# Replanning the attention half of a fused attention and expert kernel, with the first pair's rotation and the weight words in PSUM

## The chip, the cores and the metric

One core of a Trainium2 chip runs one program. Its engines are TensorE (PE in the profile), VectorE (DVE), ScalarE (ACT), GpSimd (POOL) and SyncE (SP), which here only issues transfers. The metric is the device time of one execution in microseconds; lower is better.

## What is computed

Attention over 4 sequences, 8 heads, 576 tokens and 64 columns a head, with rotated q and k, then two expert layers on the 2304 tokens of 512 columns. Everything is in fp32.

```
q_rot, k_rot = rotate(q), rotate(k)          # x1*cos - x2*sin, x1*sin + x2*cos
scores = (q_rot @ k_rot.T) / 8
attn   = exp(scores - max);  attn = attn / (sum(attn) + 1e-9)
x = (attn @ v)                               # heads side by side: 2304 x 512
x = (silu(x @ w_gate) * (x @ w_val)) @ w_out # d_ff 1536
out = relu(x @ w_in)**2 @ w_out2             # d_ff 2048
```

The host hands over q and k transposed, pair by pair, with a second copy whose halves are swapped, and a table of cosines and signed sines, so that a rotation is two products and a sum.

## The kernel before

The work has two parts. The first is attention: 16 pairs of heads (`NG`, four pairs for each of four sequences), with the first two of twelve chunks of the first expert layer done for three of the five token blocks in between, as filler for TensorE. The second part is the rest of the two expert layers; its instructions are ordered by the framework, from the loops at L749 to L812.

Precision. A product in fp32 is made of three products of a high and a low half (`mm3`, L261). The high half is a rounded copy (type fp32r), the low one the difference. For scores, k is split into `kh` and `kl`, q into `qa` (high half in a head's own 64 partitions, low half in the other 64) and `qz` (high half, zeros elsewhere), so a score tile of 128 queries and half of the 576 keys is two matmuls.

One pair g goes through these steps:

- `add_prep` (L450): SP loads q and k into `rot` (four buffers) and v. GpSimd multiplies both copies by the table in one operation of 1152 columns (L467) and adds the halves (L468). Pair 0 is done on VectorE instead, in two halves of 288 tokens (`PARTS`), and its loads carry rank -1000 so that they come first.
- `add_kq` (L481): pair 0 is split by ScalarE (L494, L499), VectorE (L495, L500) and GpSimd (L503). For later pairs ScalarE rounds (L509), GpSimd subtracts (L511), and transfers issued by SP place the pieces (L523).
- `add_scores` (L525): nine tiles of scores into PSUM (`s`, two buffers), each followed by VectorE's row maximum (L549) and ScalarE's exponential with row sums (L551). The ninth tile holds the last 64 tokens of both heads.
- `add_values` (L555): TensorE transposes the exponentials (L572) into `pt` (two PSUM buffers), ScalarE or VectorE copies them out (L564, L566), TensorE multiplies by v into `av` (L605, L608). The ninth tile is divided by its sums before it is transposed: GpSimd adds 1e-9 (L578), VectorE takes the reciprocal (L579), GpSimd scales (L580). The others are divided after the product, through a transposed copy of the reciprocals (L616, L625, L627). The result is split into high and low (L633, L635).
- `add_weight` (L648): six weight tiles are loaded raw as 64-bit words and unpacked to fp32 by `unpack_steps` (L218): ScalarE scales the upper word (L221), VectorE shifts the lower word (L222), joins the two (L223) and adds the sign (L224), ScalarE rounds (L225), GpSimd subtracts (L226). L222 to L224 work between the SBUF tiles `wa` and `wp`. The second part unpacks its 62 tiles by the same function.
- `add_filler` (L671): for three token blocks, two chunks of the first expert layer, accumulated in the one PSUM bank `mm` (L680).

The order. All these are handed to `Plan` as operations with an engine, an estimate in ns, what they read and write, and a rank. `Plan.order` (L89) runs a list schedule over the engines with those estimates: an engine that is idle takes the ready operation of lowest rank, buffers of a ring (`places`) are taken as they come free, and what comes out is the order in which the instructions are emitted. On each engine they then run in that order, a late one holding those behind it. A rank is the pair's number plus an offset for its kind (`RANK`, L21); `RANK0` adds to it for the first four pairs and is empty. For TensorE the estimates are doubled where the plan takes the clock to be halved (L162), `STAY` is what a change between scores and transposes costs in rank and `SWITCH` in ns. SP's issues are planned as operations too, with a fixed time to landing (`hold`). Before all this, VectorE and GpSimd clear some tiles (L411 to L420). The scaled table `csq` (L712) is made by ScalarE with rank -900.

## Time and profile before

| | us |
|---|---|
| median of three runs | 1168.81 |
| lowest and highest | 1167.99, 1169.2 |
| the profiled execution | 1169.47 |
| its span, first to last instruction | 1167.6 |

| engine | busy us of the span | share |
|---|---|---|
| TensorE matmuls | 1113.6 | 95% |
| TensorE weight loads | 930.4 | 80% |
| VectorE | 577.5 | 49% |
| GpSimd | 520.5 | 45% |
| ScalarE | 478.2 | 41% |

The shares are means over two parts that have different limits, so they are read by stretch. A bracket at the end of a row of the timeline holds the idle time of that engine just before it and what ended it. A row that starts with PE is a matmul; matmuls overlap, so the distance of two starts tells the pace, not the length of one.

### The profile page before, as it was taken

To read this page: it belongs to the slowest core of one execution; us is meant where nothing else is said; L and a number is where in the kernel's file an instruction comes from. 1 tells how busy PE (TensorE), PEld (TensorE's weight loads), DVE (VectorE), ACT (ScalarE), POOL (GpSimd) and SP (SyncE) were. 2 spreads that over 40 slices of the span, in tenths; PEclk is the share of its full clock that TensorE was granted. 3 is DMA by queue.
4 is the path that set the end of the run, shared out by engine and by line. 5 is a ranking of instruction groups with operands and counts; after the bars stand their busy time and mean duration, and the time that the engine had idled before them with its cause. 6 is when DMAs were issued, how large, how long until landed. Compare 5 with 4: busy or idle time off the path is not lost.

```text
span 1167.6 us, 16632 instructions
## 1 busy us (share of the span) xinstructions
PE 1113.6 (95%) x6336; PEld 930.4 (80%) x6336; DVE 577.5 (49%) x920; ACT 478.2 (41%) x980; POOL 520.5 (45%) x434
## 2 busy tenths in 40 slices
PE   2788999999999999999999999999999999999998
PEld 2666777778787888888888888888888888888886
DVE  6787555556653664635537355471144236233222
ACT  4567656666664532313223133353353224223121
POOL 4999866867423442313223134472244234224121
PEclk9999999999999999999999999999999999999999
DMA  8665566564424830202102021020021013000112
GB/s 272 191 164 166 165 166 187 149 192 121 105 83 136 315 104 25 90 1 73 36 19 91 1 72 36 19 91 1 1 89 57 1 36 91 1 1 1 64 28 73
DMA packets 61105, 102.45 MB, mean 88 GB/s; under 512 B 11104, under 2 KB 37216, under 8 KB 60128
## 3 DMA queue, kind: packets, MB, share of 16 engines
q1 hardware_dynamic: 60448, 97.18, 28.1%
q0 software_dynamic: 576, 4.19, 1.0%
q8 instruction: 50, 0.82, 0.3%
q14 instruction: 31, 0.25, 0.1%
HBM read 67.17 MB, written 12.06 MB: 68 GB/s over the span
## 4 chain that ended last, share of the span: by engine, by line
PE 77%; POOL 9%; DMA 5%; DVE 3%; issue 2%; ACT 2%; SPq 1%; POOLq 0%; DVEq 0%; ACTq 0%
PE mm L262 22%; PE mm L263 22%; PE mm L264 21%; POOL rot L467 4%; PE pt L572 3%; PE mm L680 3%; PE av L605 3%; PE s L543 3%; DMA rot<-in_k_dram 2%; POOL rot L468 2%; SPq L523 1%; DMA v<-in_v_dram 1%; DVE wp L223 1%; POOL kl L511 1%; ACT p L551 1%
## 5 line engine op out<-in xcount | busy, mean ns | idle before, releaser
L277 POOL TENSOR_TENSOR h<-s,h 128x512 fp32r<-128x512 f32 (+1 forms) x80 | 96.2, 1202 | 181.5 <-ACT h L276 178.5
L277 POOL TENSOR_TENSOR h<-hf,h 128x512 fp32r<-128x512 f32 (+1 forms) x54 | 66.5, 1231 | 151.0 <-ACT h L276 150.9
L543 PE MATMUL s<-kh,qa 128*128 128x288 f32 x320 | 95.7, 331 | 35.1 <-ACT p L551 21.5
L296 DVE TENSOR_TENSOR s<-r,mm 128x512 f32<-128x512 f32 (+1 forms) x80 | 50.6, 632 | 147.0 <-POOL h L277 75.1
L549 DVE TENSOR_REDUCE nm<-s 128x1 f32<-128x576 f32 x144 | 105.7, 752 | 32.1 <-PE s L543 30.0
L551 ACT ACTIVATE p<-s,nm 128x576 f32<-128x576 f32 x144 | 105.6, 736 | 33.4 <-DVE nm L549 31.0
L263 PE MATMUL mm<-wo,h 128*128 128x512 f32 x288 | 110.8, 389 | 0.0
L572 PE MATMUL pt<-ident,p 128*128 128x128 f32 (+1 forms) x720 | 103.8, 280 | 7.3 <-POOL p L580 3.4
L262 PE MATMUL mm<-wo,h 128*128 128x512 f32 x288 | 109.5, 389 | 0.0
L572 PEld LDWEIGHTS pt<-ident,p 128*128 128x128 f32 (+1 forms) x720 | 81.0, 137 | 23.9 <-issue 6.0
L226 POOL TENSOR_TENSOR wi<-wa,wi 128x512 fp32r<-128x512 f32 x36 | 47.1, 1309 | 108.9 <-ACT wi L225 108.9
L543 PEld LDWEIGHTS s<-kh,qa 128*128 128x128 f32 x320 | 60.9, 197 | 42.0 <-ACT p L551 27.3
L223 DVE SCALAR_TENSOR_TENSOR wp<-wa,wp 128x512 uint32<-128x512 uint32 x68 | 64.0, 942 | 61.1 <-ACT wa L221 61.0
L264 PE MATMUL mm<-wo,h 128*128 128x512 f32 x288 | 93.2, 389 | 0.0
L294 ACT ACTIVATE r<-mm 128x512 f32<-128x512 f32 (+1 forms) x80 | 43.8, 548 | 116.6 <-PE mm L264 116.0
L566 DVE COPY pc<-pt 128x512 f32<-128x512 f32 (+1 forms) x102 | 67.9, 682 | 42.7 <-PE pt L572 41.9
L285 DVE SCALAR_TENSOR_TENSOR th<-th,mm 128x512 f32<-128x512 f32 (+1 forms) x54 | 33.8, 627 | 105.9 <-ACT th L283 105.9
L543 PE MATMUL s<-kl,qz 128*128 128x288 f32 x288 | 83.7, 305 | 1.2 <-DVE kl L495 1.2
L276 ACT ACTIVATE h<-s 128x512 fp32r<-128x512 f32 (+1 forms) x80 | 47.1, 589 | 79.4 <-DVE s L296 79.4
L605 PE MATMUL av<-pc,v 128*64 128x256 f32 x640 | 76.1, 384 | 0.0
L264 PE MATMUL mm<-h,wo 128*128 128x512 f32 (+1 forms) x200 | 72.6, 369 | 0.0
L263 PE MATMUL mm<-h,wo 128*128 128x512 f32 (+1 forms) x200 | 72.6, 368 | 0.0
(198 smaller groups left out, 2780.2 us busy)
## 6 DMA issues: line engine op xcount, KB each, us to landing
raw<-in_moe_w_out_dram SPq DMA_DIRECT2D x26, 512.0 KB, 3.5
rot<-in_k_dram SPq DMA_DIRECT2D x15, 576.0 KB, 4.6
rot<-in_q_dram SPq DMA_DIRECT2D x15, 576.0 KB, 3.8
kh<-rot SPq DMA_DIRECT2D x60, 144.0 KB, 2.5
raw<-in_moe_w_in_dram SPq DMA_DIRECT2D x16, 512.0 KB, 3.6
raw<-in_moe_w_gate_dram SPq DMA_DIRECT2D x10, 512.0 KB, 3.5
raw<-in_moe_w_val_dram SPq DMA_DIRECT2D x10, 512.0 KB, 3.5
qa<-rot SPq DMA_DIRECT2D x30, 144.0 KB, 2.6
```

What stands on the lines that cost most here:

```text
L223: lambda: nc.vector.scalar_tensor_tensor(out=p(), in0=a(), scalar=3, in1=p(), op0=ALU.logical_shift_left, op1=ALU.bitwise_or),
L262: nc.tensor.matmul(ps, lhsT=ah, rhs=bh, start=first, stop=False)
L263: nc.tensor.matmul(ps, lhsT=ah, rhs=bl, start=False, stop=False)
L264: nc.tensor.matmul(ps, lhsT=al, rhs=bh, start=False, stop=last)
L277: nc.gpsimd.tensor_tensor(out=h[:, 1, :n], in0=hf[:, :n], in1=h[:, 0, :n].bitcast(F32), op=ALU.subtract)
L296: nc.vector.tensor_tensor(out=s[:, :n], in0=r[:, :n], in1=a, op=ALU.mult)
L543: nc.tensor.matmul(ps()[:, i, :HS], lhsT=a, rhs=w, start=y == 0, stop=y == len(prods) - 1)
L549: plan.add("DVE", 755, lambda ps=ps, nm=nm: nc.vector.tensor_reduce(out=nm(), in_=ps()[:, :, :HS], axis=AX.XY, op=ALU.max, negate=True), [ ...
L551: plan.add("ACT", 930, lambda x=x, ps=ps, nm=nm, p=p: nc.scalar.activation(p().rearrange("p (a b) -> p a b", a=2), ps()[:, :, :HS], AF.Exp ...
L566: nc.vector.tensor_copy(dst()[:kk], pt()[:kk, :n])
L572: nc.tensor.matmul(pt()[:kk, off + n * 128:off + n * 128 + 128], lhsT=p()[:, c * 128:c * 128 + kk], rhs=ident, is_transpose=True)
L605: nc.tensor.matmul(av()[h * 64:h * 64 + 64, 0:256], lhsT=vt()[:, h, c], rhs=pcs[c]()[:, h * 256:h * 256 + 256], start=c == 0, stop=c == 4)
```

## The change

Seven things are altered, all in the first part.

1. The rotation of pair 0 is three operations for each of q and k and each half: a product within `rot`, a product into PSUM (`pt` for k; `av` and `mm` for q), and a sum in PSUM. ScalarE and VectorE split k and q from there.
2. A dummy exponential on a tile that GpSimd clears is issued on ScalarE before the plan. The making of `csq` also waits for the last high piece of q (head 1, second half).
3. The table is loaded through ScalarE's queue. Pair 1's q and k get rank -9000 on SP, right behind pair 0's.
4. In `add_weight` the tile `p` is the PSUM bank `mm` in place of `wp`. The second part's `load_split` keeps `wp`.
5. The ninth tile's scaling is done by ScalarE or VectorE, as the plan picks, in place of GpSimd. So is the copy of `av` (L619), and pair 1's rotation may go to VectorE (`SHARE`).
6. A transpose takes the SBUF buffer of its copy at the same time (`claim`).
7. The plan: the model of TensorE's clock is gone; operations with `port` wait in the plan for one another between VectorE and GpSimd; transfers land by a rate (`RATE`, `LAND`); some estimates change; and all ranks are new, with `RANK0` for the first four pairs and `RANK1` for the first two.

```diff
-RANK = dict(ld=9.786, rope=-1.966, k=-2.118, lo=-1.665, dup=3.173, v=-2.497, s=-5.055, mx=-3.798, ex=-1.062, pt=-4.839, hi=-0.71, av=1.151, rec=-0.195, x=29.148, out=-3.224, fin=-38.149, scale=-8.913, w=0.449, dw=0.542, fill=-3.274, df=4.236)
-RANK0 = dict()
+RANK = dict(ld=176.169, rope=77.556, k=133.052, lo=-64.241, dup=130.669, v=-12.083, s=27.238, mx=100.534, ex=60.673, pt=-5.142, hi=45.754, av=95.071, rec=-6.745, x=179.568, out=-4.367, fin=-49.53, scale=-159.05, w=28.595, dw=27.25, fill=63.17, df=5.551)
+FIRST = dict(rope=((-997, -1000), (-995, -999)), k=((-998.5, -995.9), (-998, -995.8)), q=((-996.9, -995.7), (-994.9, -994.8)))
+SHARE = (1,)
+RANK0 = dict(ld=-0.835, rope=-50.984, ...)
+RANK1 = dict(ld=53.997, rope=-27.634, ...)
...
-    SWITCH = 54
-    STAY = 13.92
+    SWITCH = 80
+    STAY = 67.654
...
-                    if eng == "PE":
-                        if int((now + self.PHASE) / self.TICK) > tick:
...
-                        ns *= 1 if full else 2
+                    if ops[i]["port"] and eng == "DVE" or eng == "Pool":
+                        ns += max(0, held["Pool" if eng == "DVE" else "DVE"] - now)
+                        held[eng] = now + ns
+                    if ops[i]["size"]:
+                        moved = max(moved, now + self.LAND) + ops[i]["size"] / self.RATE
+                        hold = moved - now - ns
...
+        first = sm.tile([128, 1], F32, name="first", bufs=1)
+        nc.gpsimd.memset(first, 0.0)
+        nc.scalar.activation(first, first, AF.Exp)
...
+                    if g == 0 and i == 1:
+                        plan.add("ACT", 600, lambda c0=c0, c1=c1: nc.scalar.dma_start(out=cs()[:, :, c0:c1], in_=rope[:, :, c0:c1]), [], [(cs, n)], -1e4 + n, size=1024 * w)
+                    plan.add("SP", 600, lambda ...: nc.sync.dma_start(out=x()[:, :, c0:c1], in_=(q, k)[i][b, j][:, :, c0:c1]),
+                             [], [(x, n)], (-1e4 + n + 0.1 * (1 - i) if g == 0 else -9e3 if g == 1 else g + rk("ld", g) + 0.1 * (1 - i)), size=1024 * w)
...
+                        at0 = FIRST["rope"][n][i]
+                        y = buf("pt", [128, 512], bufs=2, pool=pp) if i else buf(("av", "mm")[n], [128, 512], pool=pp)
+                        for e in range(2):
+                            o = (lambda x=x, c0=c0, c1=c1: x()[:, 0, c0:c1]) if e == 0 else (lambda y=y, w=w: y()[:, :w])
+                            plan.add("DVE", dve(w, 150), lambda ...: nc.vector.tensor_tensor(out=o(), in0=x()[:, e, c0:c1], in1=cs()[:, e, c0:c1], op=ALU.mult),
+                                     [(cs, n)] + ([] if e == 0 else [(x, n)]), [(x, n)] if e == 0 else [y], at0, port=True)
+                        plan.add("DVE", dve(w, 150), lambda ...: nc.vector.tensor_tensor(out=y()[:, :w], in0=y()[:, :w], in1=x()[:, 0, c0:c1], op=ALU.add), [(x, n)], [y], at0)
...
-                            plan.add("Pool", pool_ns(cols), lambda fn=fn: fn(nc.gpsimd), csk if i else [csq], [(x, n)], at + 0.01 * (1 - i))
+                        ways = [("Pool", pool_ns(cols), lambda fn=fn: fn(nc.gpsimd))]
+                        if g in SHARE:
+                            ways.append(("DVE", dve(cols, 100), lambda fn=fn: fn(nc.vector)))
+                        plan.add_any(ways, csk if i else [csq], [(x, n)], at + 0.01 * (1 - i), port=True)
...
-            plan.add("Pool", 900, lambda: nc.gpsimd.tensor_scalar(pr(), pr(), rr(), None, ALU.mult), [rr], [pr], at)
+            plan.add_any([("ACT", 680, lambda: nc.scalar.activation(pr(), pr(), AF.Copy, scale=rr())),
+                          ("DVE", 400, lambda: nc.vector.tensor_scalar(pr(), pr(), rr(), None, ALU.mult))], [rr], [pr], at, port=True)
...
-            raw, a, p = buf("h", [128, 1024], U32, 4, hp), buf("wa", [128, 512], U32, 1, tp), buf("wp", [128, 512], U32, 1, tp)
+            raw, a, p = buf("h", [128, 1024], U32, 4, hp), buf("wa", [128, 512], U32, 1, tp), buf("mm", [128, 512], U32, pool=pp)
...
-        plan.add("ACT", act(2 * S), lambda: nc.scalar.activation(csq(), cs(), AF.Copy, scale=0.125), csk, [csq], -900)
+        plan.add("ACT", act(2 * S), lambda: nc.scalar.activation(csq(), cs(), AF.Copy, scale=0.125), csk + [(pair[0]["qa"], (1, 0, 1))], [csq], -900)
```

The ranks that the prediction speaks of are those of `RANK`: on TensorE `s` for scores, `pt` for transposes, `av` for the products with v, `fill` for the filler (to which four for each sequence and a step of up to `df` are added).

## Rows read from the trace of the kernel before

**Rows 1.** Busy time by stretch, the whole span but its last 6 us.

```profile
core 0: us, PE busy (x) PEld busy (x) DVE busy (x) ACT busy (x) POOL busy (x), PEclk, DMA share, GB/s
0.00:13.16 13.16, 0.00 (x0) 0.00 (x0) 7.27 (x16) 4.15 (x7) 2.62 (x12) 1.00 0.81 257
13.16:30.00 16.84, 9.53 (x36) 7.87 (x36) 13.12 (x20) 10.26 (x25) 11.82 (x11) 1.00 0.78 270
30.00:53.00 23.00, 16.88 (x150) 13.69 (x148) 16.13 (x21) 12.26 (x29) 21.38 (x14) 1.00 0.81 217
53.00:70.30 17.30, 13.56 (x83) 11.66 (x84) 15.00 (x22) 12.01 (x29) 14.92 (x12) 0.80 0.50 130
70.30:130.00 59.70, 52.74 (x446) 41.98 (x444) 44.98 (x71) 41.94 (x101) 57.19 (x46) 1.00 0.62 175
130.00:372.70 242.70, 232.19 (x1859) 190.46 (x1859) 140.85 (x249) 150.76 (x357) 140.56 (x122) 0.99 0.51 140
372.70:1161.60 788.90, 788.35 (x3770) 664.71 (x3768) 339.24 (x525) 246.86 (x440) 272.05 (x222) 1.00 0.16 53
```

**Rows 2.** TensorE's waits up to 380 us: total us, times, longest.

```profile
PE s L543 <- ACT p L551: 21.5, 16, 4.5
...
PE pt L572 <- POOL p L580: 3.4, 3, 1.7
```

**Rows 3.** The chain that ended last: start us, us, what; four and eight score matmuls.

```profile
55.89 0.90 PE s L543 x4
...
152.33 1.06 PE s L543 x8
```

**Rows 4.** Timeline of the opening, all engines: start us, us, engine, line, what.

```profile
1.50 0.59 SPq L461 DMA_DIRECT2D cs<-in_rope_dram  x1
...
4.99 0.76 DVE L467 TENSOR_TENSOR rot<-rot,cs 128x576 f32<-128x576 f32 x1 [1.30 <-DMA cs<-in_rope_dram]
...
6.75 0.76 DVE L467 TENSOR_TENSOR rot<-rot,cs 128x576 f32<-128x576 f32 x1 [1.00 <-DMA rot<-in_q_dram]
...
8.90 1.28 ACT L712 ACT_TABLE_LOAD   x1 [8.90 <-DMA cs<-in_rope_dram]
...
11.27 0.89 ACT L494 ACTIVATE kh<-rot 64x288 fp32r<-64x288 f32 x2
...
13.16 0.61 PE L543 MATMUL s<-kh,qa 128*128 128x288 f32 x1 [13.16 <-DVE qa L500]
...
19.73 2.63 POOL L467 TENSOR_TENSOR rot<-rot,cs 128x1152 f32<-128x1152 f32 x1 [2.33 <-DMA rot<-in_k_dram]
```

**Rows 5.** Timeline of VectorE and TensorE around the two largest waits.

```profile
19.79 3.12 DVE L224 SCALAR_TENSOR_TENSOR wa<-wa,wp 128x512 uint32<-128x512 uint32 x1
...
26.11 0.61 PE L543 MATMUL s<-kh,qa 128*128 128x288 f32 x1 [3.82 <-ACT p L551]
...
47.02 2.03 DVE L223 SCALAR_TENSOR_TENSOR wp<-wa,wp 128x512 uint32<-128x512 uint32 x1 [1.06 <-ACT wa L221]
...
49.08 2.98 DVE L224 SCALAR_TENSOR_TENSOR wa<-wa,wp 128x512 uint32<-128x512 uint32 x1
...
53.71 0.61 PE L543 MATMUL s<-kh,qa 128*128 128x288 f32 x1 [4.53 <-ACT p L551]
```

**Rows 6.** Durations of VectorE's lines up to 380 us: ns min/median/max.

```profile
L222 DVE TENSOR_SCALAR wp<-h x6: 414/465/1508, 15.2 to 88.3; 128x512 uint32<-128x512 uint32 x6
...
L223 DVE SCALAR_TENSOR_TENSOR wp<-wa,wp x7: 694/1904/2837, 17.5 to 356.5; 128x512 uint32<-128x512 uint32 x7
...
L224 DVE SCALAR_TENSOR_TENSOR wa<-wa,wp x7: 693/1790/3123, 19.8 to 357.2; 128x512 uint32<-128x512 uint32 x7
...
L627 DVE TENSOR_TENSOR xs<-xs,pt x32: 401/412/424, 57.0 to 373.1; 128x256 f32<-128x256 f32 x32
```

**Rows 7.** GpSimd's scaling of the ninth tile, up to 380 us.

```profile
L580 POOL TENSOR_SCALAR p<-p,rr x16: 1721/1732/1741, 39.7 to 355.4; 128x576 f32<-128x576 f32 x16
```

**Rows 8.** TensorE's groups of instructions from 320 to 372 us.

```profile
L680 PE MATMUL mm<-h,w 128*128 128x512 f32 x47 | 12.7, 405 | 0.0
```

More of the change, by code (lines that the diff above doesn't have):

```diff
@@ L60, in __init__, with add, add_any @@
         self.ops = []
-    TICK = 10240 / 3
-    COLUMNS = 3060
-    PHASE = 560
-    def add(self, eng, ns, fn, rd=(), wr=(), rank=0.0, hold=0, mode=0, share=1.0):
-        self.add_any([(eng, ns, fn)], rd, wr, rank, hold, mode, share)
-    def add_any(self, ways, rd=(), wr=(), rank=0.0, hold=0, mode=0, share=1.0):
+    LAND = 2000
+    RATE = 350
+    def add(self, eng, ns, fn, rd=(), wr=(), rank=0.0, hold=0, mode=0, port=False, size=0, claim=()):
+        self.add_any([(eng, ns, fn)], rd, wr, rank, hold, mode, port, size, claim)
+    def add_any(self, ways, rd=(), wr=(), rank=0.0, hold=0, mode=0, port=False, size=0, claim=()):
         i = len(self.ops)
@@ L84, in add_any @@
         deps.discard(i)
+        bufs += [b for b in claim if b not in bufs]
         for buf in bufs:
             buf.users += 1
-        self.ops.append(dict(ways=ways, eng=ways[0][0], ns=ways[0][1], fn=ways[0][2], deps=deps, bufs=bufs, rank=(round(rank, 6), i), hold=hold, mode=mode, cols=(ways[0][1] - 4) * 2.4 * share))
+        self.ops.append(dict(ways=ways, eng=ways[0][0], ns=ways[0][1], fn=ways[0][2], deps=deps, bufs=bufs, rank=(round(rank, 6), i), hold=hold, mode=mode, port=port, size=size))
     def order(self):
@@ L98, in order @@
         users = {}
-        ready = {}
+        ready = {eng: ([], []) for eng in ("PE", "DVE", "ACT", "Pool", "SP")}
         busy, mode = {}, {}
-        tick, counted, full = 0, 0.0, False
+        moved = 0.0
+        held = {"DVE": 0, "Pool": 0}
         events = []
@@ L522, in add_kq @@
                 for (key, src), c, dst, wr, late in moves:
-                    plan.add("SP", 450, lambda src=src, own=own, c=c, dst=dst: nc.sync.dma_start(out=raw(dst()), in_=src()[own, c]), [key], wr, at + 0.005 * late, hold=2300)
+                    plan.add("SP", 450, lambda src=src, own=own, c=c, dst=dst: nc.sync.dma_start(out=raw(dst()), in_=src()[own, c]), [key], wr, at + 0.005 * late, size=256 * (c.stop - c.start))
         def add_scores(g):
@@ L596, in add_values @@
                         pt = buf("pt", [128, 512], bufs=2, pool=pp)
[L597 removed]
+                        plan.add("PE", (4 - 3 * n) * 110, lambda n=n, pt=pt, pcr=pcr: [pcr()] + [transposes([pr], c, pt, 128 * (c % 4)) for c in (range(4), (4,))[n]], [pr], [pt], at + rk("pt", g), mode=1, claim=[pcr])
                         copy(pt, lambda n=n, pcr=pcr: pcr()[:, 512 * n:512 + 128 * n], 512 - 384 * n, 128 - 64 * n, at + rk("hi", g), [(pcr, n)])
@@ L662, in add_weight @@
             steps = unpack_steps(raw, a, p, lambda: t["w"][:, 0], lambda: t["w"][:, 1])
-            plan.add("SP", 500, load, [], [raw], at - 1, hold=4000)
+            plan.add("SP", 500, load, [], [raw], at - 1, size=524288)
             plan.add("ACT", 660, steps[0], [raw], [a], at)
-            plan.add("DVE", 700, steps[1], [raw], [p], at)
-            plan.add("DVE", 1250, steps[2], [a], [p], at)
-            plan.add("DVE", 900, steps[3], [p], [a], at)
+            plan.add("DVE", 680, steps[1], [raw, a], [p], at)
+            plan.add("DVE", 690, steps[2], [a], [p], at)
+            plan.add("DVE", 690, steps[3], [p], [a], at)
             plan.add("ACT", 630, steps[4], [a], [(wb, 0)], at)
```

67 lines of the change are left out of this document (34 added, 33 removed).

## The prediction

> **What bounds the kernel now.** I read the page's forty slices first, then the busy times by stretch, then TensorE's waits, then the timeline of the opening and of two stalls, and last the durations of single lines. The stretches [rows 1] split the span in two. From 372.7 to 1161.6 us TensorE is busy 788.35 of 788.90 us: that part (the two expert layers) is bound by TensorE's own work, and no order of other engines can shorten it. The first 372.7 us (attention, with the first expert chunks as filler) are not: TensorE stands idle 13.16 us before its first matmul, then 7.31 of 16.84, 6.12 of 23.00, 3.74 of 17.30, 6.96 of 59.70 and 10.51 of 242.70 us (each the stretch less its busy column), 47.8 us in all. Nearly two thirds of that lie before 70.3 us. The change leaves the second part's program alone, so the question is how much of these 47.8 us goes, and what new idle time comes.
>
> Two things add to it. The matmuls of the scores take 0.225 us each in a stretch of half clock (four in 0.90) and 0.13 us later (eight in 1.06) [rows 3], which are the levels 1.2 and 2.4 GHz. The stretch 53.0 to 70.3 has a granted clock of 0.80 [rows 1]: (1 - 0.80)/0.5 x 17.3 = 6.9 us at half speed, and it follows a stall of 4.53 us [rows 5]. With TensorE busy 78% of the stretch, about 2.7 us of it were lost to the clock. And the largest wait inside the part is scores waiting for an exponential to free their PSUM buffer, 21.5 us in 16 waits [rows 2]; what makes that exponential late is the next point.
>
> VectorE's two-input steps that put weight words together (L223, L224) take 0.69 us at best, 1.90 and 1.79 in the median and 2.84 and 3.12 at worst. L627 is of the same kind but has one input in PSUM, and its 32 instances lie within 401 and 424 ns though they run among the same GpSimd work [rows 6]. So an input from SBUF on both sides is what stretches, and one from PSUM is not stretched. Both large stalls of TensorE stand right behind such a step: L224 of 3.12 us at 19.79, then the scores wait 3.82 us until 26.11; L223 and L224 of 2.03 and 2.98 us at 47.02 and 49.08, then the scores wait 4.53 us until 53.71 [rows 5]. The row maximum that frees the buffer is queued behind them.
>
> **The change, part by part.**
>
> *Opening.* Before, ScalarE waits until 8.90 us for the second half of the rotation table, loads its function table (1.28 us), scales the whole table, and only at 11.27 splits k; TensorE begins at 13.16, 1.89 us later [rows 4]. The change loads the function table with a dummy exponential, moves the scaling behind the last q piece, and rotates the first pair by three half-width operations into PSUM. A 288-column operation I take at 0.45 us (L627 has 0.41 for 256 columns [rows 6]; bounds 0.38, half of the 0.76 at 4.99, and 0.76 itself [rows 4]). Rotation begins at 4.99 when the table's first half is there, so k is rotated at about 6.4 and q, which has landed by 6.75, at about 8.1. Adding the 1.89 us of before to k's gives 8.4, to q's gives 10.0; I take 9.2. Gain 4.0 (2.5 to 5). What is late next is q's rotation on VectorE. A rule speaks against part of it: the table is now issued from ScalarE's queue beside SP's, and the Trainium skill (DMA: Bandwidth & Descriptors, "Issuing engines are not separate DMA queues") says that this saves only the time of issuing, since the same 16 engines carry both. The trace can't show it, as only SP issues here. The table was issued at 1.50 us [rows 4]; issued first it could come 0.8 us earlier, by the rule hardly at all. I count nothing for it, so the sum is that of the rule; without it the sum would be 0.8 us better.
>
> *The weight words.* The intermediate word goes into TensorE's filler bank in PSUM, so L223 and L224 have one SBUF input; both should run at 0.69. The stall at 26.11 loses 3.12 - 0.69 = 2.4 us (0 to 5: the whole stall and more, or nothing if the maximum is late for another reason). The stall at 53.71 loses 5.01 - 1.38 = 3.6 (2 to 4.5). Six weights are unpacked, the last from 88.3 us (L222 [rows 6]); four are left, and by the medians each gives back 1.21 + 1.10 = 2.3 us of VectorE, 9.2 in all. VectorE is busy 60.0 of the 77.0 us from 53.0 to 130.0 [rows 1], that stretch holds 10.7 us of idle TensorE, and I let half of the 9.2 reach TensorE: 4.6 (1 to 8). The half clock behind the second stall goes with it: 2.5 (0 to 3). L222, which now writes to PSUM, has no row with that destination; between its 0.41 minimum and the 0.69 of a two-input step I take 0.69, 1.5 us over six weights, hidden under the 1.2 us a step that is saved beside it. The Trainium skill (VectorE: DVE Perf Modes, "Why PSUM operands drop a tier") speaks against this move: an operand in PSUM bars the double rate that a one-input step on fp32 has in SBUF. The 0.41 us for 512 columns is such a rate; by the rule the step takes about 0.69, which is what I count, and by the bare minimum the sum would be 1.5 us of VectorE better. The bank is shared with the filler's accumulator, so an unfinished weight holds back filler and the other way round; the first filler needs the weights anyway, and I count nothing.
>
> *Loads.* The second pair's q and k go ahead of four transfers of v and four of weights on SP. GpSimd waited for them until 19.73 us [rows 4]. The first pair, the table and the second pair are 2.95 MB (five tensors of 128 x 1152 fp32); at the 257 to 270 GB/s of the opening [rows 1] they are there after 11 to 12 us, so GpSimd may begin some 8 us earlier, and VectorE may take a share of that rotation. v and the weights come later by as much as those transfers take; the first filler is far off. Of the 13.4 us idle between 13.16 and 53 the two stalls explain some 7.6; I let 2.0 of the rest go (0 to 4).
>
> *The last tokens' scaling.* GpSimd spends 1.73 us on each of 16 [rows 7], and transposes wait 3.4 us for it in three places [rows 2]. On ScalarE or VectorE it is one pass of 576 columns, between 0.4 (half the rate's best, above) and 0.76 us (the row maximum's order of size); at 0.7 the waits shrink by 60%: 2.0 (0 to 3.4). The 27.7 us (16 x 1.73) come off GpSimd and 16 x 0.6 = 10 go onto two engines that are busy 237 and 231 of the first 372.7 us (the stretches of rows 1 added up, 64 and 62%); hidden, as long as they aren't the bound of a pair.
>
> *The new order.* All queues of the first part are replanned with other ranks, and the plan's own idea of TensorE's clock is dropped. No row shows what that does to the 10.51 us idle between 130 and 372.7. Bounds: +6 (half of it goes) and -8 (the idle share of 70.3 to 130, 11.7%, against 4.3% now, over 110 us of it). I take 1.5. For what the changes add (VectorE working on the second pair's rotation beside GpSimd, which are two-input steps in SBUF and so of the stretched kind; more copies) I take off 1.5 (0 to 4).
>
> **Sum:** 4.0 + 2.4 + 3.6 + 4.6 + 2.5 + 2.0 + 2.0 + 1.5 - 1.5 = 21.1 us. The profiled execution took 1169.47 us (span 1167.6 and 1.9 around it); less 21.1 that is 1148.4. The median of the runs shown is 0.66 lower than the profiled one, so 1147.7, rounded to 1148.
>
> **Rivals.**
>
> 1. *Supply-bound early pairs.* The stalls go, but the first four pairs are held by ScalarE and VectorE together (from 53.0 to 70.3 VectorE is busy 15.00 of 17.30, from 70.3 to 130 GpSimd 57.19 of 59.70 [rows 1]). Then only the opening and the two stalls show: 4.0 + 2.4 + 3.6 less the 1.5, or 8.5 us: 1168.8 - 8.5 = 1160. Against it: GpSimd loses the 1.73 us steps, VectorE the stretched ones. Chance 0.20.
>
> 2. *The replanned order also fills the late gaps.* The late terms go to their upper ends: 6 in place of 1.5 at the end, 8 in place of 4.6 for the weights, 3.4 in place of 2.0 for the scaling, 30.4 us in all: 1138. For it: the waits are between engines that each have slack. Chance 0.10.
>
> 3. *Filler spent too soon, slower.* The filler's rank now lies behind scores and transposes and ahead of every product with v, whatever the pair, so it is used up as soon as there is a gap. Before, the last third of it ran behind 320 us (47 matmuls of the down step alone there [rows 8]) and it covers that end. If the last two pairs run without filler they fall back to the idle shares without it: 11.7% (70.3 to 130) to 26.6% (30 to 53) of about 45 us, 5 to 12 us. Alone that doesn't make the kernel slower; it does where the early terms come to less than about 8 us as well, because the static order is wrong about when things land. Then 1168.8 - 7 + 12 = 1174. Chance 0.10.
>
> 4. *No change.* The early queue is held by ScalarE's exponentials, and each wait removed comes back at the next: 1168. Chance 0.05.
>
> **How the numbers follow.** The forecast has 0.55 and its own range of 1140 to 1156. To hold the time 8 times in 10 the range takes in nearly all of the first rival and most of the second: 1134 to 1163. It leaves out the slower one, no change and the tails. A time counts as the same within 0.2%, 2.3 us, which is about what a measurement of this kernel can tell. Faster: 0.55 + 0.20 + 0.10 = 0.85; slower 0.10; same 0.05.
>
> **What would show it.** After the change L223 and L224 of the first part should lie near 0.69 us throughout, as L627 does; if they still vary to 2 us, the reading of the stretch is wrong. TensorE's first matmul should stand near 9.2 us and no table load at 8.90. No wait of over 3 us of scores for an exponential should be left between 13 and 70 us, and no half clock after the opening. The transposes' wait for GpSimd's scaling should be gone. The end of the attention part, 372.7 before, should be near 352, and what follows should keep its 789 us with TensorE full. I am wrong if the opening is held by something that isn't in the trace of before (a later landing of the table, ScalarE's queue blocked behind its dummy function), if the first part shows new waits of TensorE behind 130 us, or if the second part gets idle time because its first weights come late.

## The result and the profile after

The changed kernel takes 1152.57 us in the median (1151.21 to 1153.01) beside 1169.01 for the kernel before on the same chip, a ratio of 0.9857 [0.9840, 0.9874]: 16.4 us less. The profiled execution took 1151.21 us (its span is 1149.4), 18.3 less than the 1169.47 of before. The forecast was 1148 and a gain of 21.1 on the profiled execution; the time lies inside the range, 4.6 us above the forecast.

The stretches of the changed kernel, cut where those of [rows 1] were, the first at its first matmul and the attention part at its own end:

```profile
core 0: us, PE busy (x) PEld busy (x) DVE busy (x) ACT busy (x) POOL busy (x), PEclk, DMA share, GB/s
0.00:10.76 10.76, 0.00 (x1) 0.01 (x1) 7.38 (x19) 4.42 (x10) 3.36 (x13) 1.00 0.82 292
10.76:30.00 19.24, 13.64 (x62) 11.58 (x64) 15.48 (x25) 13.50 (x30) 15.23 (x12) 1.00 0.94 291
30.00:53.00 23.00, 18.34 (x148) 15.29 (x145) 16.06 (x29) 14.58 (x32) 18.45 (x15) 0.93 0.80 224
53.00:70.30 17.30, 16.73 (x148) 13.83 (x147) 13.70 (x26) 12.91 (x30) 16.53 (x15) 1.00 0.64 182
70.30:130.00 59.70, 55.17 (x449) 43.88 (x448) 40.74 (x74) 39.23 (x92) 44.04 (x36) 0.97 0.62 176
130.00:354.00 224.00, 217.43 (x1771) 180.16 (x1770) 141.45 (x259) 145.61 (x339) 117.19 (x109) 1.00 0.49 139
354.00:1142.90 788.90, 787.84 (x3766) 664.29 (x3766) 338.06 (x523) 247.40 (x440) 272.42 (x222) 1.00 0.17 54
```

The attention part ends at 354.0 us, 18.7 earlier. Of the 788.90 us cut behind it TensorE is busy 787.84, and from there to the end of the span it is 795.4 us, 794.9 before. Idle time of TensorE (stretch less busy column) is 10.76 before the first matmul, then 5.60, 4.66, 0.57, 4.53 and 6.57: 32.7 us where [rows 1] had 47.8. That is 15.1 of the 18.7; the other 3.6 are busy time (321.3 us in the five columns, 324.9 before). Between 53.0 and 70.3 the granted clock is 1.00 where it was 0.80, but between 30 and 53 it is 0.93 where it was 1.00. The clock column can't be relied on for the first matmuls: it reads 1.00 from the start in both kernels, but the score matmuls begin 0.24 us apart until 25.6 us (until 28.0 before) and 0.13 apart after that, and in [rows 3] such a pace belongs to half clock.

TensorE's waits up to 380 us, in the columns of [rows 2]:

```profile
PE s L565 <- DVE qa L522: 10.8, 1, 10.8
PE s L565 <- ACT p L573: 7.7, 12, 2.4
PE pt L594 <- DVE pc L588: 6.6, 7, 3.5
```

Scores wait 7.7 us for exponentials, 21.5 before, and the wait for GpSimd's scaling is gone. In their place transposes wait 6.6 us for VectorE's copies, half of it in one wait of 3.5.

VectorE's steps on the weight words, ns min/median/max, to be read beside [rows 6]:

```profile
L227 DVE TENSOR_SCALAR mm<-h x6: 684/695/717, 20.5 to 144.7; 128x512 uint32<-128x512 uint32 x6
L228 DVE SCALAR_TENSOR_TENSOR mm<-wa,mm x6: 682/695/697, 21.3 to 145.4; 128x512 uint32<-128x512 uint32 x6
L229 DVE SCALAR_TENSOR_TENSOR wa<-wa,mm x6: 655/672/686, 22.0 to 149.2; 128x512 uint32<-128x512 uint32 x6
```

All three lie between 655 and 717 ns; the joins went up to 2837 and 3123.

The opening, from the timeline of all engines (start, length, engine, line; idle before and its end in brackets), beside [rows 4]:

```profile
2.06 1.28 ACT L429 ACT_TABLE_LOAD   x1 [2.06 <-issue]
...
5.10 0.46 DVE L481 TENSOR_TENSOR rot<-rot,cs 128x288 f32<-128x288 f32 x1 [1.41 <-DMA rot<-in_k_dram]
...
8.16 0.45 DVE L516 TENSOR_TENSOR kl<-pt,kh 64x288 fp32r<-64x288 f32 x1 [0.33 <-ACT kh L515]
...
8.90 0.45 DVE L483 TENSOR_TENSOR av<-av,rot 128x288 f32<-128x288 f32 x1
...
9.38 0.83 ACT L521 ACTIVATE qa<-av 64x288 fp32r<-64x288 f32 x2 [1.25 <-DVE av L483]
...
10.76 0.61 PE L565 MATMUL s<-kh,qa 128*128 128x288 f32 x1 [10.76 <-DVE qa L522]
```

The table load is out of the way at 2.06, rotation starts at 5.10 and waits for k, and the first matmul is at 10.76 (13.16 before). The sum of q that it needs (L483 into `av`) runs only at 8.90: in VectorE's order the two products of k's second half (7.38 and 8.54) and a `kl` that waits for ScalarE (8.16) stand ahead of it.

The one stall of over 3 us that is left behind the opening, from the same view:

```profile
44.93 2.61 POOL L487 TENSOR_TENSOR rot<-rot,csq 128x1152 f32<-128x1152 f32 x1 [3.23 <-issue]
...
47.62 0.22 POOL L637 TENSOR_SCALAR rs<-sums 128x4 f32<-128x4 f32 x1
47.88 0.18 DVE L638 RECIPROCAL rs<-rs 128x4 f32<-128x4 f32 x1 [3.79 <-POOL rs L637]
...
47.98 1.26 DVE L588 COPY pc<-pt 128x512 f32<-128x512 f32 x2
...
48.69 0.66 PE L594 MATMUL pt<-ident,p 128*128 128x128 f32 x4 [3.54 <-DVE pc L588]
```

GpSimd waits 3.23 us and rotates q of the fourth pair (index 3) for 2.61 (its row names no releaser here; in two runs below, n_recip and n_noadd, the same rotation waits for the load of q); a 0.22 us addition on four sums is queued behind that; VectorE stands 3.79 us before the reciprocal that needs it, with the copies of the transposes behind; TensorE waits 3.54. The half clock between 49.7 and 53.1 follows.

### The profile page after: what moved, and what is told of

Its sections match the earlier page's. It is cut to its first block, busy times and chain, and to the rows that moved or that the text cites. A ratio compares the mean times of both kernels' runs of the same rounds, so it can differ in the third digit from the quotient of the medians.

```text
span 1149.4 us, 16627 instructions
## 1 busy us (share of the span) xinstructions
PE 1110.1 (97%) x6336; PEld 929.5 (81%) x6336; DVE 574.4 (50%) x953; ACT 477.6 (42%) x970; POOL 487.2 (42%) x417
## 4 chain that ended last, share of the span: by engine, by line
PE 77%; POOL 8%; DMA 5%; DVE 3%; SPq 2%; ACT 2%; issue 2%; POOLq 0%; DVEq 0%; ACTq 0%
PE mm L267 22%; PE mm L268 22%; PE mm L269 22%; PE s L565 3%; PE pt L594 3%; POOL rot L487 3%; PE av L628 3%; PE mm L704 2%; SPq L545 2%; POOL rot L488 1%; DMA rot<-in_k_dram 1%; DMA qa<-rot 1%; DMA v<-in_v_dram 1%; DMA rot<-in_q_dram 1%; POOL kl L533 1%
## 5 line engine op out<-in xcount | busy, mean ns | idle before, releaser
L571 DVE TENSOR_REDUCE nm<-s 128x1 f32<-128x576 f32 x144 | 104.6, 749 | 21.2 <-PE s L565 20.1
L573 ACT ACTIVATE p<-s,nm 128x576 f32<-128x576 f32 x144 | 105.7, 737 | 20.3 <-DVE nm L571 18.7
L594 PE MATMUL pt<-ident,p 128*128 128x128 f32 (+1 forms) x720 | 101.4, 279 | 10.4 <-DVE pc L588 6.6
L228 DVE SCALAR_TENSOR_TENSOR wp<-wa,wp 128x512 uint32<-128x512 uint32 x62 | 53.4, 862 | 58.4 <-ACT wa L226 58.4
L281 ACT ACTIVATE h<-hf 128x512 fp32r<-128x512 f32 (+1 forms) x54 | 31.5, 583 | 98.9 <-DVE hf L293 98.4
```

The costliest lines, as they stand in the source:

```text
L228: lambda: nc.vector.scalar_tensor_tensor(out=p(), in0=a(), scalar=3, in1=p(), op0=ALU.logical_shift_left, op1=ALU.bitwise_or),
L281: nc.scalar.activation(h[:, 0, :n], hf[:, :n], AF.Copy)
L571: plan.add("DVE", 755, lambda ps=ps, nm=nm: nc.vector.tensor_reduce(out=nm(), in_=ps()[:, :, :HS], axis=AX.XY, op=ALU.max, negate=True), [ ...
L573: plan.add("ACT", 930, lambda x=x, ps=ps, nm=nm, p=p: nc.scalar.activation(p().rearrange("p (a b) -> p a b", a=2), ps()[:, :, :HS], AF.Exp ...
L594: nc.tensor.matmul(pt()[:kk, off + n * 128:off + n * 128 + 128], lhsT=p()[:, c * 128:c * 128 + kk], rhs=ident, is_transpose=True)
```

## The experiments

Each kernel ran beside the kernel before on one chip. A price is the difference of two ratios times 1169 us; with the two intervals put together, one of under about 2.5 us (3 to 4 for u_fill and n_recip) isn't told from nothing. Where the text says "orders kept", each engine's list is that of the changed kernel, and only the edited operation differs.

**u_words: the intermediate word back in SBUF, orders kept.**

```diff
-            raw, a, p = ..., buf("mm", [128, 512], U32, pool=pp)
+            raw, a, p = ..., Buf("mm", lambda: tp.tile([128, 512], U32, tag="wp", name="wp"))
```

> The changed kernel with one part undone: the intermediate weight word p lies in SBUF again (tile wp), while every engine's order stays that of the changed kernel. Theory A (the forecast's terms): VectorE's two joining steps (0.69 us each in the changed kernel's trace) stretch again to about 2 us each where GpSimd works beside them, and the row maxima queued behind them come late; 2.4 + 3.6 + 4.6 + 2.5 us were counted for this, so the time rises from 1152.6 to about 1160 to 1166. Theory B (the order carries the gain): the new ranks put the weight words where VectorE has slack, so the steps stretch but TensorE hardly sees it: 1152 to 1155. Tell-tale row: durations of the two joining lines, and a wait of scores for an exponential of over 2 us right behind one of them.

1165.46 us, ratio 0.9972 [0.9960, 0.9985]: 13.4 us. The same lines of VectorE, then two of TensorE's waits:

```profile
L227 DVE TENSOR_SCALAR wp<-h x6: 418/1638/2033, 21.9 to 158.4; 128x512 uint32<-128x512 uint32 x6
L228 DVE SCALAR_TENSOR_TENSOR wp<-wa,wp x8: 679/959/2992, 23.9 to 377.8; 128x512 uint32<-128x512 uint32 x8
L229 DVE SCALAR_TENSOR_TENSOR wa<-wa,wp x8: 685/1098/3114, 26.9 to 378.6; 128x512 uint32<-128x512 uint32 x8
```

```profile
PE s L565 <- ACT p L573: 12.9, 12, 5.6
...
PE pt L594 <- DVE pc L588: 10.0, 8, 3.5
```

The stretch is back in all three steps, the one-input shift among them (418 to 2033 ns), and both waits behind VectorE grow. The only thing that differs is where the word lies, so in this order the 13.4 us are shown to come from that.

**u_scale: the ninth tile's scaling back on GpSimd, orders kept.**

```diff
-            plan.add_any([("ACT", 680, lambda: nc.scalar.activation(pr(), pr(), AF.Copy, scale=rr())),
-                          ("DVE", 400, lambda: nc.vector.tensor_scalar(pr(), pr(), rr(), None, ALU.mult))], ...)
+            on_pool = lambda: nc.gpsimd.tensor_scalar(pr(), pr(), rr(), None, ALU.mult)
+            plan.add_any([("ACT", 680, on_pool), ("DVE", 400, on_pool)], ...)
```

> The changed kernel with one part undone: the ninth tile of each pair is scaled by GpSimd again, at the place in the order that ScalarE or VectorE had for it. Theory A: the transposes of the ninth tile wait for 1.73 us in place of 0.52 to 0.78 and GpSimd has 27.7 us more to do; 2.0 us were counted, so 1154 to 1156. Theory B: GpSimd's load in the first 130 us is what holds the supply of later pairs, then more comes back: over 1158. Rival: hidden, 1152 to 1153.

1155.06 us, 0.9888 [0.9873, 0.9903]: 3.6 us. Transposes wait 1.4 us in one place for the scaling; scores wait 10.1 us for exponentials in place of 7.7, which points to work queued behind GpSimd for a part of the price.

**u_open: no dummy exponential, and `csq` made ahead of the first `kh`.**

```diff
-        first = sm.tile([128, 1], F32, name="first", bufs=1)
-        nc.gpsimd.memset(first, 0.0)
-        nc.scalar.activation(first, first, AF.Exp)
...
+            seq = plan.order()
+            fn = seq.pop(seq.index(marks["csq"]["fn"]))
+            seq.insert(seq.index(marks["kh"]["fn"]), fn)
```

> The changed kernel with one part undone: no dummy exponential, and the scaled table is made by ScalarE ahead of its first piece of k, as before. All other orders stay. Theory A: the function table (1.28 us) and the scaling (1.16 us) stand ahead of the first k piece again, and the scaling waits for the table's second half; TensorE's first matmul moves from 10.76 to about 13 us and the time rises by about 2 to 3 us, to 1155. Theory B: the first pair's scores are held by VectorE, not by the start, so the later start is taken up by 30 us: 1153.

1155.79 us, 0.9890 [0.9876, 0.9905]: 3.9 us. The first matmul stands at 14.34, 3.58 later than after the change, and the price is about that.

**u_loads: q and k of the second pair (index 1) behind the first four transfers of v and of weights.**

```diff
...
+            ahead = [o["fn"] for o in sorted(early, key=lambda o: o["at"])]
+            for fn in ahead:
+                seq.remove(fn)
+            at = min(seq.index(o["fn"]) for o in late)
+            seq[at:at] = ahead
```

> The changed kernel with one part undone: the second pair's q and k are loaded behind four transfers of v and four of weights again. Theory A: GpSimd's first rotation moves from 9.66 to about 17 us, the second pair's scores come late, and 2 to 6 us are lost: 1155 to 1159. Theory B: the second pair has that much slack: 1152 to 1154.

1158.45 us, 0.9910 [0.9894, 0.9927]: 6.2 us. Timeline of GpSimd and TensorE:

```profile
18.15 2.61 POOL L490 TENSOR_TENSOR rot<-rot,cs 128x1152 f32<-128x1152 f32 x1 [15.10 <-DMA rot<-in_k_dram]
20.70 1.32 POOL L532 CAST qz<-qa 64x288 fp32r<-64x288 f32 x2
...
21.18 0.61 PE L572 MATMUL s<-kl,qz 128*128 128x288 f32 x1 [9.57 <-POOL qz L532]
```

The first matmul isn't touched (11.00). The second needs the first pair's `qz`, which in GpSimd's order stands behind the second pair's rotation, and that waits for its load until 18.15: TensorE stands 9.57 us. So in this order an early load decides the first pair as well, and the 6.2 us hold a wait that the kernel before didn't have: there the first pair's `qz` ran ahead of the second pair's rotation.

**u_ranks: the changed operations and planner, with the old `RANK`, `STAY` and `SWITCH`.**

```diff
-RANK = dict(ld=176.169, rope=77.556, ...)
+RANK = dict(ld=9.786, rope=-1.966, ...)
-RANK0 = dict(ld=-0.835, ...)
-RANK1 = dict(ld=53.997, ...)
+RANK0 = dict()
+RANK1 = dict()
-    SWITCH = 80
-    STAY = 67.654
+    SWITCH = 54
+    STAY = 13.92
```

> The changed kernel with its operations, its planner and the first pair's places, but planned with the ranks of before (RANK of before, no RANK0 and RANK1, STAY 13.92, SWITCH 54). Theory A (the forecast): the operations carry the gain and the ranks were counted at 1.5 us, so 1152 to 1156. Theory B (the search for ranks carries much of it): the time goes back by 5 us or more, to 1157 to 1165, with new waits of TensorE behind 70 us.

1176.59 us, 1.0067 [1.0051, 1.0083]: 24.5 us, and slower than before. The first wait of TensorE's list and two of the stretches, in the columns above:

```profile
PE s L565 <- ACT p L573: 20.1, 17, 3.9
```

```profile
70.30:130.00 59.70, 53.06 (x399) 42.55 (x397) 36.03 (x67) 34.72 (x81) 36.45 (x32) 0.91 0.54 151
130.00:354.00 224.00, 207.32 (x1624) 170.13 (x1624) 143.55 (x255) 132.02 (x311) 119.75 (x105) 0.96 0.50 139
```

The time lies beyond both theories. All other parts of the change are there, with the weight words in PSUM, yet scores wait 20.1 us for exponentials. Up to 70.3 us TensorE has been busy 47.5 us, 48.7 in the changed kernel, so little is lost by then. Behind 130 us 16.7 of 224.0 us are idle at a clock of 0.96 (6.6 at 1.00 in the changed kernel), and the last transposes of attention start at 378.95, 353.66 in the changed kernel. The old ranks were made for the old planner, so this run shows old ranks under the new planner; the new planner alone was not separated from them.

**u_rot: the first pair's rotation in SBUF, orders kept.**

```diff
-                        y = buf("pt", [128, 512], bufs=2, pool=pp) if i else buf(("av", "mm")[n], [128, 512], pool=pp)
+                        y = Buf("pt" if i else ("av", "mm")[n], lambda n=n, i=i: ap.tile([128, HS], F32, name=f"y{i}{n}"))
```

> The changed kernel with one part undone: the first pair's second product and its sum lie in SBUF in place of PSUM, three operations as now, orders unchanged. Theory A: GpSimd stands idle until 9.66 us, so the first half isn't stretched; of the second half some VectorE operations have two SBUF inputs beside GpSimd's first rotation of 2.6 us and wait for it once or twice: 0 to 3 us, 1152 to 1155. Rival: ScalarE and VectorE read SBUF no slower than PSUM, and nothing is seen: 1151 to 1153.

1152.70 us, 0.9865 [0.9850, 0.9879]: 0.9 us, not told from nothing.

**d_words: the kernel before, with only the word in PSUM and the estimates 680, 690 and 690 for the three steps.**

```diff
-            raw, a, p = ..., buf("wp", [128, 512], U32, 1, tp)
+            raw, a, p = ..., buf("mm", [128, 512], U32, pool=pp)
...
```

> The kernel before with one part alone: the intermediate weight word in the filler's PSUM bank, the three estimates 680, 690 and 690, planned with its own ranks and clock model. Theory A: the two stalls of before (3.82 and 4.53 us) and the half clock shrink as counted (13.1 us in all, and the undoing cost about 13.8 us against the changed kernel's ratio), so 1154 to 1160. Theory B (the part pays only in the new order, since the bank is shared with the filler): 1162 to 1169, with the filler and the weights waiting for one another behind 75 us.

1166.15 us, 0.9983 [0.9974, 0.9992]: only 2.0 us gained, though the two joins there are at 677 to 697 ns throughout. The order is planned anew with the old ranks. The fourth pair's last product stands at 107.5 us, 9 us earlier than before, the sixth pair's at 155.7, 7.7 earlier; then this, from the timeline of ScalarE and TensorE:

```profile
174.75 0.60 ACT L707 ACTIVATE ys<-mm 128x512 f32<-128x512 f32 x1 [2.51 <-DMA ypart<-ys]
...
175.40 1.65 PE L680 MATMUL mm<-h,w 128*128 128x512 f32 x3 [3.55 <-ACT ys L707]
```

ScalarE can't copy the filler's bank out before its output buffer has been stored, TensorE's next filler waits for the bank, and 6.8 us of half clock follow. The seventh pair's last product is 5.4 us earlier than before, and the attention part ends at 368.5, 4.2 earlier. So about half of what was won by 107 us is lost again, some 2 us of it over this stall; where the rest goes was not traced.

**n_recip: the addition of 1e-9 moved from GpSimd to VectorE, right ahead of the reciprocal.**

```diff
-                plan.add("Pool", 110, lambda ...: nc.gpsimd.tensor_scalar(rs(), sums()[...], 1e-9, None, ALU.add), rd, [rs], at)
+                plan.add("Pool", 110, lambda: None, rd, [rs], at)
-                plan.add("DVE", 180, lambda ...: nc.vector.reciprocal(out=rs(), in_=rs()), [], [rs], at)
+                plan.add("DVE", 180, lambda ...: (nc.vector.tensor_scalar(rs(), sums()[...], 1e-9, None, ALU.add), nc.vector.reciprocal(out=rs(), in_=rs())), [], [rs], at)
```

> Not an undoing: the changed kernel, but the small addition of 1e-9 ahead of each reciprocal is done by VectorE right before it, in place of GpSimd; orders otherwise unchanged. In the changed kernel's trace VectorE waits 3.8 us at 47.9 for that addition, which stands on GpSimd behind a rotation that waits for its load, and TensorE waits 3.54 us behind VectorE; a stretch of half clock follows at 49.7. Theory A: that wait was the cause, and with the addition on VectorE it goes: 2 to 5 us less, 1147 to 1150. Theory B: TensorE would have waited at the same place for the third pair's supply (the same late load), and 48 more VectorE operations cost: 1152 to 1155.

The ninth tile's addition on one column is moved in the same way. 1151.85 us, 0.9849 [0.9822, 0.9876]: no difference that can be told. Timeline of GpSimd, VectorE and TensorE, then the durations of the addition on four columns and of the reciprocal:

```profile
46.19 2.63 POOL L487 TENSOR_TENSOR rot<-rot,csq 128x1152 f32<-128x1152 f32 x1 [4.48 <-DMA rot<-in_q_dram]
...
47.10 1.75 DVE L638 TENSOR_SCALAR rs<-sums 128x4 f32<-128x4 f32 x1
...
50.36 0.74 PE L594 MATMUL pt<-ident,p 128*64 128x128 f32 x4 [2.50 <-DVE pc L588]
```

```profile
L638 DVE TENSOR_SCALAR rs<-sums x32: 150/163/2672, 40.9 to 344.5; 128x4 f32<-128x4 f32 x32
L638 DVE RECIPROCAL rs<-rs x32: 177/178/180, 41.8 to 344.7; 128x4 f32<-128x4 f32 x32
```

The addition no longer waits in GpSimd's queue, but beside GpSimd's rotation it takes 1.75 us in place of 0.16, and at worst 2.67. The stall shrinks from 3.54 to 2.50 and nothing of it reaches the end.

**n_noadd: the addition of 1e-9 left out of the computation.**

```diff
-                plan.add("Pool", 110, lambda ...: nc.gpsimd.tensor_scalar(rs(), sums()[...], 1e-9, None, ALU.add), rd, [rs], at)
+                plan.add("Pool", 110, lambda: None, rd, [rs], at)
-                plan.add("DVE", 180, lambda ...: nc.vector.reciprocal(out=rs(), in_=rs()), [], [rs], at)
+                plan.add("DVE", 180, lambda ...: nc.vector.reciprocal(out=rs(), in_=sums()[...]), [], [rs], at)
```

> The changed kernel without the addition of 1e-9 ahead of the reciprocals (left out of the computation; a row's sum of exponentials is at least 1, where 1e-9 is below the last bit of fp32). VectorE takes the reciprocal from the sums themselves, GpSimd has 48 operations less, and orders are otherwise unchanged. With the addition moved to VectorE the wait at 47.9 us stayed, because one 4-column addition there took 1.75 us beside a GpSimd rotation. Theory A: now nothing on VectorE waits for GpSimd at that place, the 3.54 us wait of TensorE and the half clock behind it shrink, and 2 to 5 us are gained over the changed kernel: ratio 0.981 to 0.984, 1147 to 1150. Theory B: the third pair's rotation, late by its load, holds TensorE some us later anyway: less than 1.5 us gained, 1151 to 1152.

The ninth tile's addition is left out as well. 1151.87 us, 0.9864 [0.9849, 0.9878]: no gain. Timeline of GpSimd, ScalarE and TensorE:

```profile
45.76 2.63 POOL L487 TENSOR_TENSOR rot<-rot,csq 128x1152 f32<-128x1152 f32 x1 [4.72 <-DMA rot<-in_q_dram]
...
49.89 0.68 ACT L531 ACTIVATE rot<-rot 128x576 fp32r<-128x576 f32 x1 [4.37 <-POOL rot L488]
...
50.96 0.73 ACT L573 ACTIVATE p<-s,nm 128x576 f32<-128x576 f32 x1
...
51.84 0.61 PE L565 MATMUL s<-kh,qa 128*128 128x288 f32 x1 [3.21 <-ACT p L573]
```

VectorE waits for nothing there now, and TensorE still stands 3.21 us: ScalarE has the rounding of the same pair's q ahead of the exponential, and that waits 4.37 us for the same late rotation. One late load held two queues, and freeing one shows the other. (The pair is the fourth; the expectation calls it the third.)

**u_all: the changed kernel's order, with words, scaling, opening and loads undone together** (the edits of u_words, u_scale, u_open and u_loads).

> The order of the changed kernel on every engine, but four parts undone at once: the weight word in SBUF, the ninth tile scaled by GpSimd, no dummy exponential with the scaled table ahead of the first k piece, and the second pair's loads behind v and four weights. Undone one by one they cost 13.8, 3.4, 4.1 and 6.8 us against the changed kernel (by the ratios to the kernel before). Theory A (their prices add): 28 us more, about 1180, slower than the kernel before by some 11: the new order is then worth nothing without the parts it was planned for. Theory B (the order alone carries a gain): below 1168.

1174.12 us, 1.0059 [1.0042, 1.0075]: 23.6 us above the changed kernel, where the four single prices add up to 27.1, and 6.9 above the kernel before: between the two theories. The 3.5 between 23.6 and 27.1 is not told from nothing by these intervals. What is left of the change in this run is more than the order: the first pair's rotation in PSUM (u_rot), the other copy taken off GpSimd, the shared rotation, `claim` and the new planner; apart from u_rot these were not undone singly.

**d_open: the kernel before with the dummy exponential, and `csq` made behind the first pair's last `qa`.**

```diff
+        first = sm.tile([128, 1], F32, name="first", bufs=1)
+        nc.gpsimd.memset(first, 0.0)
+        nc.scalar.activation(first, first, AF.Exp)
...
+            seq = plan.order()
+            fn = seq.pop(seq.index(marks["csq"]["fn"]))
+            seq.insert(seq.index(marks["qa"]["fn"]) + 1, fn)
```

> The kernel before with one part alone: a dummy exponential loads the function table early, and the scaled table is made behind the last piece of q in place of ahead of the first piece of k; everything else keeps its order. Theory A (the forecast's first term): TensorE starts at about 9.5 us in place of 13.16 and the time falls by 3 to 4 us, to 1164 to 1165. Theory B (a fixed order gives an early start back): TensorE starts early, but the row maxima stand in the order behind the weight words, which wait for their load until about 16 us, so the first exponential stays at 18 to 19 us and the time stays within 1.5 us of before, 1167 to 1168.5.

1168.02 us, 1.0000 [0.9990, 1.0009]: nothing, though the first matmul is at 11.31 in place of 13.16. Timeline of VectorE, ScalarE and TensorE:

```profile
17.67 0.69 DVE L224 SCALAR_TENSOR_TENSOR wa<-wa,wp 128x512 uint32<-128x512 uint32 x1
...
23.40 0.68 ACT L515 ACTIVATE rot<-rot 128x576 fp32r<-128x576 f32 x1 [4.31 <-POOL rot L473]
23.98 0.72 ACT L557 ACTIVATE p<-s,nm 128x576 f32<-128x576 f32 x1
...
24.85 0.61 PE L549 MATMUL s<-kh,qa 128*128 128x288 f32 x1 [4.67 <-ACT p L557]
```

The word step (L224) takes 0.69 us here and is done at 18.4, and still the scores wait 4.67 us, until 24.85 (26.11 before). The exponential that they wait for is in ScalarE's order behind the rounding of the second pair's k, which waits 4.31 us for GpSimd's rotation and so for that pair's load. The start is given back as theory B says, though not at the place that it names.

**u_fill: the changed kernel, planned with the filler's rank at 110 in place of 63.17,** behind the products with v.

```diff
-RANK = dict(..., fill=63.17, df=5.551)
+RANK = dict(..., fill=110, df=5.551)
```

> The changed kernel planned anew with one rank other: the filler at 110 in place of 63.17, so that it comes behind the products with v and not ahead of them. Theory A (the forecast's third rival turned round): filler ahead of those products costs nothing at the end, since the last block's filler can't finish before the third sequence is done, and behind them it only fills later gaps: within 2 us, 1150 to 1154. Theory B (any plan with other ranks is another draw, and the given ranks were picked out of many): 4 us or more slower, over 1156, with new waits at places that have nothing to do with filler.

1181.71 us, 1.0121 [1.0100, 1.0142]: 30.9 us slower. TensorE's timeline, then ScalarE's:

```profile
357.12 0.38 PE L649 MATMUL pt<-ident,rb 128*128 128x128 f32 x2
...
367.69 2.93 PE L704 MATMUL mm<-h,w 128*128 128x512 f32 x6 [2.52 <-ACT ys L731]
377.41 2.93 PE L704 MATMUL mm<-h,w 128*128 128x512 f32 x6 [6.79 <-ACT ys L731]
...
383.52 0.39 PE L267 MATMUL mm<-x3h,w 128*128 128x512 f32 x1
```

```profile
375.91 0.68 ACT L226 ACTIVATE wa<-raw 128x512 f32<-128x512 f32 x1 [2.35 <-DMA raw<-in_moe_w_gate_dram]
376.76 0.60 ACT L731 ACTIVATE ys<-mm 128x512 f32<-128x512 f32 x1 [0.16 <-DMA ypart<-ys]
```

The last transposes of attention are only 3.5 us later (357.12; 353.66 after the change). The loss lies behind them, and not in places that have nothing to do with filler, as theory B has it: the filler that is left, 24 matmuls of the down step among it, has nothing to hide its own waits. Its last three groups of six wait for the one bank `mm`, up to 6.79 us; that wait is ScalarE's, whose copy of the bank stands in its order behind a weight step that waits for a load until 375.91. From 367.6 to 383.5 the granted clock is 0.59 as well. The second part starts at 383.52 in place of 354.55.

## Why the prediction was right, and where it was not

**What was read rightly.** The part that bounds and the part that doesn't: the second part kept its time, and the whole gain lies ahead of 354 us, where 352 was forecast. Within it the idle time of TensorE fell by 2.4 us before the first matmul, by 3.2 from there to 53 us, 3.2 to 70.3, 2.4 to 130 and 3.9 behind that, where the forecast had only 1.5 for the order. The joins are near 0.69 us throughout, and undoing the weight words alone costs 13.4 us; the four terms for them came to 13.1. That these agree is in part luck: the terms were worked out from the kernel before, where the same part brings 2.0 (d_words), and the 13.4 take in the shift, which in SBUF stretches to 1638 ns in the median (u_words) and was counted as 1.5 us lost by the change. The trace could bear that because one line of the same kind with an input in PSUM stood beside it [rows 6]. On the shift, which now writes to PSUM, the Trainium skill (VectorE: DVE Perf Modes, "Why PSUM operands drop a tier") agrees with the trace: 684 to 717 ns, where the SBUF form had 414 at best. The opening was counted at 4.0, and undoing two of its parts (the dummy exponential and the later `csq`) costs 3.9, again in the new order alone. Its steps were less right: k's sum ended at 6.4 as forecast, but q's at 9.35 and not 8.1, so the first matmul is at 10.76 and not 9.2; what was missed is that the order lets three steps that the first matmul doesn't need go ahead of q's sum. Compared with the kernel before, the first matmul comes 2.4 us earlier; the 3.58 that u_open shows hold for the new order. Issuing the table from another queue gave nothing: rotation starts at 5.10 (4.99 before) and waits for k.

**Mis-sized: the loads.** Counted 2.0 (0 to 4), measured 6.2 by u_loads, a price that holds a wait of this order's own. The stall at 26.11 was given wholly to the long L224 (2.4 us). d_open shows a second limit right behind that one: with L224 at 0.69 the exponential came only 1.3 us earlier (23.98; 25.25 before), as the second pair's rotation was late. The trace of before had that row, from the timeline of ScalarE:

```profile
24.66 0.68 ACT L509 ACTIVATE rot<-rot 128x576 fp32r<-128x576 f32 x1 [1.08 <-POOL rot L468]
25.25 0.72 ACT L551 ACTIVATE p<-s,nm 128x576 f32<-128x576 f32 x1
```

A rounding waits for GpSimd's rotation just ahead of that exponential; the prediction followed the wait one step back, to VectorE, and stopped there. So a part of what was put down to words is a gain of loads and words together, and the two prices can't be taken apart at that stall.

**Mis-sized: the scaling.** Counted 2.0 (0 to 3.4), measured 3.6, at the edge of what can be told from it. The price of the new operations was right: seven on ScalarE at 777 ns and nine on VectorE at 520 in the median make 10.1 us, as forecast. The term was worked out from the transposes' wait alone; that 27.7 us off GpSimd also let the work queued behind it go sooner fits the longer wait for exponentials in u_scale, but was not shown by itself.

**Failed: the order as a term of its own.** It was counted at +1.5, with bounds of +6 and -8; what was found lies near the lower bound. By u_all the new order with four of the operations as they were is 6.9 us slower than before; by u_ranks the new operations with the old ranks are 7.8 us slower than before. Only together are they faster, by 16.7 (1 less the ratio of 0.9857, times 1169). The same shows from the other side: under the old ranks the words alone bring 2.0 and the opening alone nothing, while in the new order undoing them costs 13.4 and 3.9. So the step that failed is the sum itself. It added each part's price as if the rest stayed as it was, and there is no such price: -6.9 for the order and +23.6 for the four parts on it give the measured 16.7. The forecast had 0 for the order and the additions together (+1.5 - 1.5) and 21.1 for the four parts. So one comes from 21.1 to 16.7 by -6.9 for the order, +5.8 for loads and scaling, +0.2 for words and opening, and -3.5 for what the four parts share (27.1 singly, 23.6 together, a difference within the noise). That the forecast came near is in part luck, errors of both signs.

**Half clock and new stalls.** No half clock was forecast behind the opening, and there is some: 0.93 between 30 and 53 and 0.97 between 70.3 and 130. The half clock before was read as what follows the 4.53 us stall, but it was in two pieces: the trace has 0.59 from 53.0 to 57.2, 1.00 to 66.0 and 0.60 to 70.3, and only the first stands at that stall. In the changed kernel the half clock between 30 and 53 stands behind the stall at 48.69, which the prediction's test (scores waiting for an exponential) didn't cover, since transposes wait there for copies. The cause of that stall, the late q of the fourth pair, is seen in n_recip and n_noadd; that removing one of its two ways to TensorE gains nothing is shown, what removing the late load itself would gain wasn't tried.

**The rivals.** The range of 1134 to 1163 took in supply-bound pairs (1160) as well, so the time alone would not decide. The row does: between 53.0 and 70.3 TensorE is busy 16.73 of 17.30, so the pairs are not supply-bound there. The late gaps closed in part (6.57 idle of 224.0; 10.51 of 242.7 before), short of the second rival. The third, filler spent too soon, did not come about: in the changed kernel filler (L704) still starts at 352.16, 24 matmuls of the down step behind 320 us. u_fill ranks it later and loses 30.9 us, nearly all behind the attention, where filler is left over and nothing hides its waits. That is one other rank; whether one between the two, or an earlier one, would do better was not tried.

## What to carry to other kernels

Price a change to operations and a change to their order together: run the new operations in the old order, and the old ones in the new order, before either is credited. When a stall has a cause, look for the next wait in the same queue just behind it, since two late things can stand one behind the other, as in d_open and n_noadd, and then freeing one gains nothing. Filler that waits for loads and for a single bank is better not left over: in u_fill it cost most of 30.9 us where no other work hid its waits.

## What was not expected of the hardware

A VectorE operation on four columns and one SBUF input (n_recip's addition, 128x4) takes 150 ns alone and up to 2672 ns beside GpSimd, while the reciprocal of the same shape never takes over 180. Where it is long it ends with GpSimd's operation: the one at 47.10 ends at 48.85, GpSimd's rotation at 48.82. The same addition on one column doesn't stretch, though several of its instances (at 33.09 and 54.32, for two) ran inside a subtraction of GpSimd; its durations in the same kernel:

```profile
L601 DVE TENSOR_SCALAR rr<-sums x16: 143/146/155, 33.1 to 346.6; 128x1 f32<-128x1 f32 x16
```

The Trainium skill (SBUF — State Buffer, "Who interferes with whom") puts one-input scalar operations among those that can take the ports shared with GpSimd; the row agrees, 2672 ns, and shows it for an operation as short as this. Why one column is exempt no run here tells.
